# One attention and feed-forward kernel, its commands split finer and their order and engines set anew

## The chip, the cores and the metric

The kernel runs on one core of one Trainium2 chip. The metric is the device time of one execution in microseconds (us), lower is better. A profiled execution gives a span, from the first to the last instruction, and a trace of every instruction and DMA packet.

The engines have queues of their own and each works in order: TensorE (PE, with weight loads listed apart as PEld), VectorE (DVE), ScalarE (ACT), GpSimd (POOL) and SyncE (SP), which only issues DMAs. POOL issues DMAs too: those that convert float32 to float16 on the way.

## The reference, cut to what matters

```python
# q, k, v: (4 batches, 8 heads, 768 tokens, 64) float32; is_retrieval = [1,0,1,0,0,0,1,0]
scores = q @ k.T / 8                       # per batch and head
mask = causal                              # retrieval heads
mask = causal & (first 4 keys | last 64 keys)   # the other heads
a = softmax(where(mask, scores, -1e9))
x = (a @ v), heads side by side            # (3072 tokens, 512)
h = max(x @ w1, x @ w2, x @ w3)            # 512 -> 768
out = h @ w_out                            # 768 -> 512, float32
```

## The kernel before

The work is cut by batch `b` (4) and half of the tokens (2 halves of 384): eight chunks. A chunk has two attention groups `t` of four heads (`t = 4b + 2*half + qd`), each of two pairs `i` of heads. After both groups of a chunk its feed-forward part (FFN) may run: 18 products (three weights, six column blocks, four matmuls each) and 3 output groups.

The order is written out by hand. `PROGRAM` is a list of short commands, which a loop at the end of the kernel runs through; each puts its instructions on the queues of its engines, and nothing reorders them afterwards. Data dependences become semaphore waits. So a command's place sets its place in each queue that it touches, and a letter in it chooses the engine: `d` DVE, `a` ACT, `p` POOL. The commands:

- `hl half hp n ss`: loads K and Q of `n` head pairs of batch 0 as float32 (line 187, two heads each DMA), on SP. `load_v b half` loads V in three DMAs on SP (287). `load b qd` loads K and Q of four heads of a later batch on POOL, to float16 (251). `w i` loads a weight (403, 410) on POOL; w0 comes in two halves.
- `cast half hp` turns batch 0's K and Q of a pair to float16 (212); `turnp` transposes them on PE (231) and copies them out of PSUM (239). For later batches `turn b qd i part` transposes K (`i` = 0) or Q (1) on DVE (267), four commands for each four heads.
- `v t i`: casts V of a pair to `va` (504) and writes `vf`, V times the retrieval flag of its head (506). For far key blocks the product takes `vf`, which is zero for a head that doesn't see them.
- `s t u`: scores of a unit `u` (553; two units in a first half, four in a second; for batch 0 often one pair at a time) and the exponential on ACT (564), which writes `pt`. The scores' PSUM has two buffers `sps`. In `t` 0 and 1 masks are added by matmuls with the identity (537).
- `k t i u`: multiplies the diagonal blocks of `pt` by a mask table (586). `em` and `m` write these tables (389), `flags`, `read` and `far` the flags of the heads.
- `av t i`: A times V (602), then reciprocal (610) and scaling (612) on DVE. With `D` the result is transposed by a DMA on SP (621); otherwise `x t i` does it on PE and copies it (638). The `x` of a chunk's last pair also puts its FFN in the queue.
- `f n`: the next step of the FFN at the head of the queue: one product (438) with its eviction (copy 455 on the engine named if it is the first weight's, else a maximum on DVE, 458), or one output group (474), copied on the engine named (480) and stored (481). Behind each output group the generator yields twice, so the second `f` there does nothing.
- `idle n`: matmuls on zeros at the start; `gate`: SP waits for a piece of `pt`.

All PSUM tiles but the scores' share four buffers ("bank") in turn: a product's fifth successor there waits until its own eviction is done.

Batch 0's order, in words: loads, casts and transposes of pairs as they come; `t` 0 and 1; then the FFN of its first half from 23.6 us, mixed with `t` 2 and 3; then `s 4 0`, the first scores of batch 1.

Of the kernel before, what the change touches and what calls it, by code (L numbers as in the profile page):

```python
# [10 lines left out]
FP16 = mybir.dt.float16  # L11
# [32 lines left out]
FIRST = "hl 0 0 1, ir"  # L44

PROGRAM = (
    "idle 2, idle 8, cast 0 0 aa, hl 0 1 1 ss, hl 0 2 2 ss, read, hl 1 0 2 ss, cast 0 1 pp",
    "flags, cast 0 2 ap, em 1, turnp 0 1 a, far, em 0, turnp 0 0 aa, cast 0 3 da, em 2, em 3",
    "load_v 0 0 4 4, s 0 0 1, s 0 0 0, v 1 1 pp, cast 1 1 pa, turnp 0 3 dd, turnp 0 2 da",
    "w 0 2 0, load_v 0 0 0 4, v 0 0 dp, s 1 0 0, w 0 2 1, s 0 1 0 b, hl 1 2 2 ss, s 1 0 1",  # L50
    "cast 1 2 dp, v 1 0 dd, s 0 1 1, s 1 1 0 b, av 0 0, v 0 1 pp, turnp 1 1 a, s 1 1 1",
    "turnp 1 2 aa, x 0 0 a, s 2 0 1, cast 1 0 dp, load_v 0 1, cast 1 3 ad, av 1 1, s 2 1 1",
    "av 1 0, x 1 1 d, av 0 1, turnp 1 0 ad, s 2 2 1, x 1 0 d, s 3 0 0, m 0, w 1, x 0 1 d",
    "s 2 0 0, m 3, m 1, f 1 d, f 1 d, s 2 1 0, s 2 2 0, m 2, f 1 a, f 1 d, k 2 1 2 p, k 2 0 1 d",
    "w 2, f 1 d, s 2 3 1, load 1 0, w 3, k 3 0 0 d, s 3 1 0, f 1 a, s 2 3 0, load 1 1",
    "k 2 0 3 p, k 2 0 2 p, turnp 1 3 dd, k 3 0 1 p, k 2 1 1 d, k 2 1 3 d, f 1 d, f 1 d",
    "v 2 0 ad, f 1 a, f 1 a, v 3 1 pp, f 1 d, s 3 0 1, v 2 1 dp, s 3 1 1, f 1 a, v 3 0 ap",
    "av 2 0 D, f 1 d, f 1 d, s 3 2 0, turn 1 0 0 0, turn 1 0 0 1, f 1 a, turn 1 0 1 0, s 3 2 1",
    "s 3 3 0, k 3 0 2 p, k 3 1 2 p, turn 1 0 1 1, f 1 a, av 2 1 D, s 3 3 1, k 3 1 1 d",
    "k 3 0 3 p, k 3 1 3 p, f 1 a, k 3 1 0 d, load_v 1 0, gate, f 1 a, s 4 0, k 4 1 0 p",  # L60
    "v 4 0 pp, av 3 0, av 3 1, f 1 a, f 1 a, x 3 0 d, s 4 1, turn 1 1 0 1, x 3 1 a, f 1 d",
    "v 5 1 pp, turn 1 1 1 0, turn 1 1 1 1, turn 1 1 0 0, k 4 0 1 d, k 4 0 0 d, k 4 1 1 p, f 1 a",
    "f 1 a, f 1 d, load_v 1 1, f 1 a, f 1 a, f 1 a, v 4 1 pd, f 1 a, f 1 d, s 5 0, f 1 a, f 1 d",
    "av 4 0 D, k 5 0 0 d, f 1 d, s 5 1, k 5 0 1 p, load_v 2 0, f 1 a, f 1 a, load 2 0, f 1 a",
    "s 6 0, f 1 d, av 4 1 D, f 1 a, v 5 0 ap, f 1 a, s 6 1, f 1 a, av 5 0 D, f 1 d, f 1 d",
    "k 5 1 1 p, k 5 1 0 p, v 7 0 dp, s 6 2, k 6 1 2 p, f 1 a, av 5 1 D, turn 2 0 1 0, f 1 a",
    "v 6 0 ad, s 6 3, turn 2 0 0 1, x 5 1 d, f 1 a, turn 2 0 1 1, load 2 1, load 3 1",
    "load_v 2 1, v 6 1 ap, f 1 d, f 1 d, k 6 0 2 p, v 9 0 ap, k 6 1 3 p, f 1 a, f 1 a",
    "turn 2 0 0 0, s 7 0, f 1 a, f 1 d, f 1 d, turn 2 1 0 0, k 6 0 1 d, f 1 a, s 7 1, f 1 d",
    "f 1 a, f 1 a, k 6 1 1 p, k 7 1 1 d, f 1 d, s 7 2, f 1 a, f 1 a, k 6 0 3 p, k 7 1 2 d",  # L70
    "turn 2 1 1 0, load 3 0, av 6 0 D, s 7 3, f 1 d, v 7 1 pp, av 6 1 D, k 7 1 3 p, f 1 d",
    "turn 3 1 1 0, k 7 0 3 p, turn 2 1 0 1, s 8 0, k 7 0 1 p, turn 2 1 1 1, k 7 0 2 p, f 1 a",
    "f 1 d, load_v 3 0, k 8 0 0 p, av 7 1 D, s 8 1, f 1 a, f 1 a, s 9 0, v 8 0 ap, k 8 0 1 d",
    "f 1 a, f 1 d, av 7 0 D, v 13 1 pp, s 9 1, f 1 a, av 8 0 D, f 1 d, s 10 0, f 1 a, x 7 1 d",
    "f 1 a, v 10 0 dd, f 1 d, s 10 1, f 1 a, f 1 d, v 9 1 ad, f 1 a, f 1 d, f 1 a, s 10 2",
    "f 1 d, f 1 d, f 1 d, k 8 1 0 p, f 1 d, k 9 0 0 p, k 9 1 1 d, f 1 d, f 1 d, v 11 0 ad",
    "f 1 d, k 9 1 0 p, v 12 0 ad, k 9 0 1 p, k 8 1 1 d, av 9 0 D, v 8 1 ap, s 10 3, f 1 d",
    "f 1 a, av 8 1 D, turn 3 0 1 0, s 11 0, k 10 1 1 p, f 1 d, f 1 d, k 10 0 3 p, f 1 a",
    "av 9 1 D, v 13 0 ap, f 1 a, k 10 1 3 d, turn 3 0 1 1, x 9 1 a, k 10 0 1 p, s 11 1, f 1 a",
# [30 lines left out]
def kernel(  # L110
# [68 lines left out]
    def load_pairs(half, hp, n, engines):  # L179
        for nm, src, eng in zip(("ks", "qs"), (k, q), engines):  # L180
            st = (
                pairs2.tile([P, 4, HB, D], FP32, tag=nm, name=nm) if n == 2
                else once.tile([P, 2 * n, HB, D], FP32, name=f"{nm}{hp}")
            )
            m = 2 * n if eng is nc.gpsimd else 2
            for h in range(0, 2 * n, m):
                eng.dma_start(  # L187
                    out=st[:, h : h + m],
                    in_=src[
                        0, 2 * hp + h : 2 * hp + h + m, half * HALF : (half + 1) * HALF  # L190
                    ].rearrange("h (p j) d -> p h j d", p=P),
                )
            for i in range(n):
                staged.setdefault((half, hp + i), []).append(st[:, 2 * i : 2 * i + 2])

    def load_cast(half, hp, n):
        for nm, src in (("kc", k), ("qc", q)):
            st = half16.tile([P, 4, HB, D], FP16, tag=nm, name=nm)
            nc.gpsimd.dma_start(
                out=st[:, 0 : 2 * n],  # L200
                in_=src[
                    0, 2 * hp : 2 * hp + 2 * n, half * HALF : (half + 1) * HALF
                ].rearrange("h (p j) d -> p h j d", p=P),
            )
            for i in range(n):
                cast.setdefault((half, hp + i), []).append(st[:, 2 * i : 2 * i + 2])

    def cast_pair(half, hp, engines):
        cast[half, hp] = []
        for nm, src, op in zip(("kn", "qn"), staged.pop((half, hp)), engines):  # L210
            x = half16.tile([P, HB, 2, D], FP16, tag=nm, name=nm)
            op(out=x, in_=src.rearrange("p h j d -> p j h d"))
            cast[half, hp].append(x)
# [6 lines left out]
    def turn_pair(half, hp, *engines):  # L220
        if (0, hp // 2) not in KQs:
            KQs[0, hp // 2] = qkt.tile([P, 2, S, 2], FP16, tag="KQ", name="KQ")
        xs = cast.pop((half, hp))
        n = 2 // len(engines)
        for part, op in enumerate(engines):
            tr = bank([P, 1024], FP16, "tr")
            for i in range(n):
                for j in range(HB):
                    c, x = i * HALF + j * P, xs[part + i]
                    if x.shape[1] == HB:  # L230
                        nc.tensor.transpose(
                            tr[:, c : c + P], x[:, j].rearrange("p h d -> p (h d)"), ident
                        )
                        continue
                    for h in range(2):
                        nc.tensor.transpose(
                            tr[D * h : D * h + D, c : c + P], x[:, h, j], ident
                        )
# [60 lines left out]
    def load_first(half, hp, n, e="sc"):  # L299
        by = {"s": nc.sync, "c": nc.scalar}  # L300
        load_pairs(half, hp, n, [by[x] for x in e])
# [414 lines left out]
```

## Time and profile before

| | |
|---|---|
| three runs | 200.95 us median (199.65, 200.95, 203.45) |
| the profiled execution | span 199.9 us; its last store is under way from 197.2 |
| PE, DVE, ACT, POOL busy | 190.0, 148.3, 115.9, 90.5 us |
| masks (line 586) | POOL 54, 57.3 us; DVE 32, mean 522 ns (512 elements) and 281 ns (256) |
| exponentials (line 564) | 98, 83.3 us on ACT |
| batch 0's first exponential | 9.85 us |
| first FFN product | 23.64 us |
| `s 4 0` on PE | 43.32 us |
| DMA engines busy, 5 to 45 us | all 16, nearly throughout |

The span is what the sum below is made against. Busy times are of single engines and overlap; an engine off the chain that ends last may stand idle at no cost. In the slices of the span each digit is a fortieth, 5 us, in tenths of busy time. Matmuls are pipelined: one of 384 columns is listed with 327 ns, but four in a row take 650 ns.

### The profile page before, as it was taken

The numbers are of one execution on the slowest core, as the hardware profiler recorded it, in microseconds if no ns is written. First come the engines' busy times: TensorE is split into PE (matmuls) and PEld (weight loads), VectorE is DVE, ScalarE is ACT, GpSimd is POOL, SyncE is SP. The second block draws the span as 40 slices with busy tenths as digits, with TensorE's granted clock in tenths as the row PEclk, the third lists the DMA queues.
The fourth block names the chain that finished last, engine by engine and source line by source line (L and its number), as shares of the span: only waits on it lengthen the run. The fifth ranks groups of instructions, "written<-read, shape, count | busy, mean of one in ns | idle before, by whom it ended". The sixth has DMA issues, their size and how long they took to land.

```text
span 199.9 us, 5135 instructions
## 1 busy us (share of the span) xinstructions
PE 190.0 (95%) x2059; PEld 109.3 (55%) x2059; DVE 148.3 (74%) x311; ACT 115.9 (58%) x171; POOL 90.5 (45%) x118
## 2 busy tenths in 40 slices
PE   7688898999999999999999999999999999999993
PEld 2345444565556455666456645574656455765552
DVE  3638965998976789896469998996978288767750
ACT  4489983765658798687776756634366565100011
POOL 3429187583276598490697245652010197000000
PEclk9889999999999999999999999999999999999999
DMA  5999999995979989988521232703500120124004
GB/s 143 312 245 230 196 195 212 208 169 76 283 173 211 162 169 208 218 218 176 147 76 23 43 124 74 159 20 73 167 5 20 53 108 0 23 59 157 3 0 157
DMA packets 48429, 26.48 MB, mean 132 GB/s; under 512 B 36758, under 2 KB 43926, under 8 KB 48406
## 3 DMA queue, kind: packets, MB, share of 16 engines
q1 hardware_dynamic: 43366, 17.96, 37.9%
q0 software_dynamic: 4624, 7.87, 21.9%
q8 instruction: 16, 0.26, 0.6%
q10 hardware_dynamic: 416, 0.33, 0.5%
q14 instruction: 7, 0.06, 0.1%
HBM read 25.17 MB, written 6.29 MB: 157 GB/s over the span
## 4 chain that ended last, share of the span: by engine, by line
PE 75%; DMA 11%; DVE 4%; SPq 3%; issue 2%; ACT 2%; POOL 0%; DVEq 0%
PE yy L438 39%; PE yy L474 14%; PE st L553 9%; PE oacc L602 9%; DMA vs<-in_v_dram 7%; PE yst L438 3%; DMA qs<-in_q_dram 2%; DVE KQ L267 2%; SPq L187 2%; ACT pt L564 1%; DMA xT<-x 1%; PE yst L474 1%; DVE acc L458 1%; DVE hT L458 1%; SPq L621 1%
## 5 line engine op out<-in xcount | busy, mean ns | idle before, releaser
L564 ACT ACTIVATE pt<-st 128x1024 f16<-128x1024 f32 (+3 forms) x98 | 83.3, 905 | 33.0 <-PE st L553 31.0
L586 POOL TENSOR_TENSOR pt<-pt,mk 128x512 f16<-128x512 f16 (+1 forms) x54 | 57.3, 1088 | 38.4 <-ACT pt L564 20.1
L438 PE MATMUL yy<-xT,w1t 128*128 128x384 f16 x180 | 35.8, 327 | 1.2 <-DVE pt L586 1.2
L438 PE MATMUL yy<-xT,w2t 128*128 128x384 f16 x180 | 36.1, 326 | 0.0
L438 PE MATMUL yy<-xT,w0t 128*128 128x384 f16 x180 | 35.8, 327 | 0.3
L458 DVE TENSOR_TENSOR acc<-yy,acc 128x384 f16<-128x384 f32 x45 | 24.8, 557 | 10.7 <-PE yy L438 8.6
L474 PE MATMUL yy<-woutt,hT 128*128 128x512 f16 (+1 forms) x138 | 31.6, 375 | 0.0
L553 PE MATMUL st<-KQ 32*128 32x384 f16 (+5 forms) x560 | 29.4, 281 | 1.4 <-ACT pt L564 0.8
L458 DVE TENSOR_TENSOR hT<-yy,acc 128x384 f16<-128x384 f32 x45 | 24.8, 556 | 4.5 <-PE yy L438 2.3
L602 PEld LDWEIGHTS <-pt 128*128 128x128 f16 x672 | 24.4, 97 | 4.8 <-DVE va L504 0.7
L267 DVE STREAM_TRANSPOSE KQ<-kq 128x384 f32<-128x384 f32 x24 | 25.5, 1132 | 0.6 <-DMA kq<-in_q_dram 0.6
L602 PE MATMUL oacc<-va,pt 128*128 128x65 f16 x352 | 24.9, 193 | 0.5 <-DVE va L504 0.5
L438 PEld LDWEIGHTS <-w1t 128*128 128x128 f16 x192 | 17.5, 98 | 14.1 <-issue 1.6
L438 PEld LDWEIGHTS <-w0t 128*128 128x128 f16 x192 | 17.8, 98 | 13.4 <-issue 0.8
L438 PEld LDWEIGHTS <-w2t 128*128 128x128 f16 x192 | 17.3, 98 | 11.9 <-issue 1.4
L553 PEld LDWEIGHTS <-KQ 32*128 32x128 f16 (+1 forms) x560 | 12.2, 93 | 18.8 <-issue 11.8
L474 PEld LDWEIGHTS <-hT 128*128 128x128 f16 x150 | 13.8, 98 | 14.7 <-issue 0.8
L602 PE MATMUL oacc<-vf,pt 128*128 128x65 f16 x320 | 21.1, 193 | 0.0
L455 ACT CAST acc<-yy 128x384 f16<-128x384 f32 x25 | 12.0, 481 | 13.9 <-PE yy L438 13.5
L612 DVE TENSOR_TENSOR x<-oacc,rc 128x384 f16<-128x384 f32 x32 | 17.8, 557 | 1.1
L480 DVE COPY ot<-yy 128x512 f32<-128x512 f32 (+1 forms) x15 | 10.1, 675 | 9.2 <-PE yy L474 9.2
L506 POOL TENSOR_TENSOR vf<-va,far 128x384 f16<-128x384 f16 x10 | 8.6, 867 | 17.3 <-ACT va L504 12.9
(72 smaller groups left out, 143.4 us busy)
## 6 DMA issues: line engine op xcount, KB each, us to landing
out_dram<-ot SPq DMA_DIRECT2D x23, 256.0 KB, 2.1
vs<-in_v_dram SPq DMA_DIRECT2D x21, 256.0 KB, 5.6
kq<-in_k_dram POOLq DMA_DIRECT2D x6, 384.0 KB, 7.9
kq<-in_q_dram POOLq DMA_DIRECT2D x6, 384.0 KB, 10.0
ks<-in_k_dram SPq DMA_DIRECT2D x8, 192.0 KB, 3.6
qs<-in_q_dram SPq DMA_DIRECT2D x7, 192.0 KB, 4.8
vs<-in_v_dram SPq DMA_DIRECT2D x6, 128.0 KB, 4.8
w0t<-in_moe_w_dram POOLq DMA_DIRECT2D x2, 384.0 KB, 9.4
```

Source lines behind the costliest of these rows:

```text
L267: nc.vector.transpose(out=dst.rearrange("c (p j) -> c j p", j=n)[:, j0:j1], in_=src.rearrange("c (j i) -> c j i", i=R),)
L438: nc.tensor.matmul(yy[:, 0:HALF], w_t[wi][:, ks, ni * P : (ni + 1) * P], xT[b, half][ks].rearrange("p a t -> p (a t)"), start=(ks == 0), s ...
L455: copy_out[0](out=acc[ni], in_=yy[:, 0:HALF])
L458: nc.vector.tensor_tensor(out=dst, in0=yy[:, 0:HALF], in1=acc[ni], op=ALU.max)
L474: nc.tensor.matmul(yo[:, 0:n], hT[ns][:, tb * P : (tb + 1) * P], woutt[:, ns, c : c + n], start=(ns == 0), stop=(ns == NNB - 1),)
L480: op(out=ot[:, c : c + n], in_=yo[:, 0:n])
L506: vf_engine.tensor_tensor(out=vf[j][:, hs, k0:k1, 0:D], in0=vs[:, hs, 0:1] if half == 0 else va[j][:, hs, k0:k1, 0:D], in1=far[:, hs, k0:k ...
L553: nc.tensor.matmul(sts[g // m][:, g % m, c0 : c0 + n * P], KQ[rows, 0, ki * P : (ki + 1) * P], KQ[rows, 1, t0 : t0 + n * P], start=(c0 == ...
L564: nc.scalar.activation(out=pts[t, i][:, u, h0 : h0 + m, 0:w], in_=st[:, :, 0:w], func=AF.Exp, scale=sc,)
L586: engine.tensor_tensor(out=x, in0=x, in1=m, op=ALU.mult)
L602: nc.tensor.matmul(o[:, qi, hl, 0 : D + 1], pt[:, u, hl, c : c + P], vv[:, 2 * hp + hl, ki, 0 : D + 1], start=(idx == 0), stop=(idx == len ...
L612: nc.vector.tensor_tensor(out=x, in0=o[:, :, :, 0:D], in1=rc.unsqueeze(3).to_broadcast([P, HB, 2, D]), op=ALU.mult,)
```

## The change

Loads and casts of batch 0 are now one command for K (0) or Q (1): `hl half hp n i s`, `cast half hp i engine`. `v` only casts V; the new `vf t i engine` writes the scaled copy. `k t i n` handles one entry `n` of the list of masks, where `u` named the unit after which one or two of them became due. The second yield behind an output group is gone, and with it 24 `f` commands. The first loads stand outside the list, unchanged (K of pair 0 on SP, Q on ACT's queue, then the flags). All commands are in a new order, and many have another engine. Options that the list did not use are removed.

The old list up to `s 5 0`, then the new one up to there, and the functions that differ:

```diff
...
-FIRST = "hl 0 0 1, ir"
 PROGRAM = (
-    "idle 2, idle 8, cast 0 0 aa, hl 0 1 1 ss, hl 0 2 2 ss, read, hl 1 0 2 ss, cast 0 1 pp",
-    "flags, cast 0 2 ap, em 1, turnp 0 1 a, far, em 0, turnp 0 0 aa, cast 0 3 da, em 2, em 3",
-    "load_v 0 0 4 4, s 0 0 1, s 0 0 0, v 1 1 pp, cast 1 1 pa, turnp 0 3 dd, turnp 0 2 da",
-    "w 0 2 0, load_v 0 0 0 4, v 0 0 dp, s 1 0 0, w 0 2 1, s 0 1 0 b, hl 1 2 2 ss, s 1 0 1",
-    "cast 1 2 dp, v 1 0 dd, s 0 1 1, s 1 1 0 b, av 0 0, v 0 1 pp, turnp 1 1 a, s 1 1 1",
-    "turnp 1 2 aa, x 0 0 a, s 2 0 1, cast 1 0 dp, load_v 0 1, cast 1 3 ad, av 1 1, s 2 1 1",
-    "av 1 0, x 1 1 d, av 0 1, turnp 1 0 ad, s 2 2 1, x 1 0 d, s 3 0 0, m 0, w 1, x 0 1 d",
-    "s 2 0 0, m 3, m 1, f 1 d, f 1 d, s 2 1 0, s 2 2 0, m 2, f 1 a, f 1 d, k 2 1 2 p, k 2 0 1 d",
-    "w 2, f 1 d, s 2 3 1, load 1 0, w 3, k 3 0 0 d, s 3 1 0, f 1 a, s 2 3 0, load 1 1",
-    "k 2 0 3 p, k 2 0 2 p, turnp 1 3 dd, k 3 0 1 p, k 2 1 1 d, k 2 1 3 d, f 1 d, f 1 d",
-    "v 2 0 ad, f 1 a, f 1 a, v 3 1 pp, f 1 d, s 3 0 1, v 2 1 dp, s 3 1 1, f 1 a, v 3 0 ap",
-    "av 2 0 D, f 1 d, f 1 d, s 3 2 0, turn 1 0 0 0, turn 1 0 0 1, f 1 a, turn 1 0 1 0, s 3 2 1",
-    "s 3 3 0, k 3 0 2 p, k 3 1 2 p, turn 1 0 1 1, f 1 a, av 2 1 D, s 3 3 1, k 3 1 1 d",
-    "k 3 0 3 p, k 3 1 3 p, f 1 a, k 3 1 0 d, load_v 1 0, gate, f 1 a, s 4 0, k 4 1 0 p",
-    "v 4 0 pp, av 3 0, av 3 1, f 1 a, f 1 a, x 3 0 d, s 4 1, turn 1 1 0 1, x 3 1 a, f 1 d",
-    "v 5 1 pp, turn 1 1 1 0, turn 1 1 1 1, turn 1 1 0 0, k 4 0 1 d, k 4 0 0 d, k 4 1 1 p, f 1 a",
-    "f 1 a, f 1 d, load_v 1 1, f 1 a, f 1 a, f 1 a, v 4 1 pd, f 1 a, f 1 d, s 5 0, f 1 a, f 1 d",
...
+    "hl 0 2 2 0 s, cast 0 0 1 p, idle 8, read, flags, cast 0 0 0 a, hl 0 2 2 1 s, turnp 0 0 da",
+    "em 0, hl 0 1 1 1 s, hl 1 2 2 0 s, em 3, cast 0 2 0 d, cast 0 3 1 d, cast 0 3 0 p",
+    "cast 0 2 1 p, idle 2, em 1, s 0 0 0, turnp 0 3 ad, turnp 0 2 aa, em 2, hl 1 2 2 1 s, s 1 0 1",
+    "cast 0 1 1 p, cast 1 2 0 d, s 1 0 0, cast 1 3 1 p, s 0 1 0 b, cast 1 3 0 d, load_v 0 0 0 4",
+    "hl 0 1 1 0 s, cast 1 2 1 d, hl 1 0 2 0 s, load_v 0 0 4 4, v 0 1 p, hl 1 0 2 1 s, s 1 1 1",
+    "turnp 1 2 ad, m 3, far, cast 0 1 0 p, load_v 0 1, turnp 1 3 ad, cast 1 1 0 d, v 0 0 d",
+    "s 3 0 0, vf 0 0 d, cast 1 0 1 p, s 3 2 0, cast 1 1 1 p, m 0, cast 1 0 0 d, s 3 1 0, s 3 3 0",
+    "w 0 2 0, v 1 0 a, turnp 0 1 d, v 1 1 p, s 1 1 0 b, vf 0 1 d, m 2, turnp 1 0 aa, s 0 0 1",
+    "turnp 1 1 d, s 0 1 1, vf 1 0 p, av 0 0, load 1 0, s 2 0 0, av 0 1, s 3 0 1, vf 1 1 p",
+    "k 3 0 0 p, av 1 0, k 3 0 2 p, v 2 0 p, w 0 2 1, av 1 1, s 2 3 0, s 2 2 0, x 1 0 d, s 3 2 1",
+    "x 0 0 d, x 0 1 d, v 3 0 d, x 1 1 d, w 1, s 2 1 0, s 3 1 1, k 2 0 2 d, f 1 a, k 2 0 1 d",
+    "k 3 0 3 d, turn 1 0 0 1, k 3 1 0 d, k 2 0 0 d, v 3 1 p, vf 2 0 p, m 1, k 3 0 1 d, vf 3 0 p",
+    "vf 3 1 p, s 3 3 1, v 2 1 a, turn 1 0 1 0, f 1 a, turn 1 0 1 1, f 1 a, k 3 1 2 p, s 2 0 1",
+    "k 3 1 3 d, w 2, s 2 1 1, k 3 1 1 d, av 2 0 D, av 3 0, w 3, f 1 a, s 2 3 1, s 2 2 1, gate",
+    "turn 1 0 0 0, f 1 d, vf 2 1 d, f 1 a, av 3 1, x 3 0 a, s 4 0, k 2 1 0 p, f 1 d, k 2 1 1 d",
+    "f 1 d, k 2 1 2 p, f 1 a, f 1 a, s 4 1, f 1 d, f 1 a, k 4 1 2 p, x 3 1 d, f 1 d, k 4 1 1 p",
+    "f 1 d, f 1 a, f 1 a, f 1 a, av 2 1 D, f 1 a, f 1 a, load_v 1 0, f 1 a, f 1 a, load 1 1",
+    "turn 1 1 0 0, f 1 a, turn 1 1 0 1, k 4 0 0 d, turn 1 1 1 1, k 4 0 1 d, f 1 a, f 1 d",
+    "turn 1 1 1 0, k 4 1 0 d, v 5 0 p, f 1 d, f 1 a, f 1 a, s 5 0, f 1 d, f 1 d, load_v 1 1",
...
-    def cast_pair(half, hp, engines):
-        cast[half, hp] = []
-        for nm, src, op in zip(("kn", "qn"), staged.pop((half, hp)), engines):
-            x = half16.tile([P, HB, 2, D], FP16, tag=nm, name=nm)
-            op(out=x, in_=src.rearrange("p h j d -> p j h d"))
-            cast[half, hp].append(x)
+    def cast_pair(half, hp, i, op):
+        nm = ("kn", "qn")[i]
+        x = half16.tile([P, HB, 2, D], FP16, tag=nm, name=nm)
+        op(out=x, in_=staged.pop((half, hp, i)).rearrange("p h j d -> p j h d"))
+        cast[half, hp, i] = x
...
                 eng.dma_start(out=out[r0 : r0 + P, c : c + n], in_=ot[:, c : c + n])
             yield
-            yield
...
-    def prep_v(t, i, op, vf_engine):
+    def cast_v(t, i, op):
+        b, half, qd = where(t)
+        k0 = half * HB
+        hs = slice(4 * qd + 2 * i, 4 * qd + 2 * i + 2)
+        op(out=va[b % 2][:, hs, k0 : k0 + HB, 0:D], in_=staged_v[b, half][:, hs])
+
+    def scale_v(t, i, vf_engine):
         b, half, qd = where(t)
         vs = staged_v[b, half]
-        j, k0 = b % 2, half * HB
+        j = b % 2
         hs = slice(4 * qd + 2 * i, 4 * qd + 2 * i + 2)
-        vdst = va[j][:, hs, k0 : k0 + HB, 0:D]
-        op(out=vdst, in_=vs[:, hs])
         k0, k1 = ((0, 1), (1, 4))[half]
         vf_engine.tensor_tensor(
...
-        for at, u0, nu, cols, n, m0 in APART if t in (3,) else MASKED[half]:
-            if at != u:
-                continue
-            m = mk[:, h0 : h0 + 2, m0 : m0 + n]
+        _, u0, nu, cols, n, m0 = (APART if t in (3,) else MASKED[half])[u]
+        m = mk[:, h0 : h0 + 2, m0 : m0 + n]
...
```

## The prediction

> **What bounds the kernel now.** I read the page's busy rows and slices first, to see which engine is full and where it is not.
>
> ```profile
> span 199.9 us, 5135 instructions
> PE 190.0 (95%) x2059; PEld 109.3 (55%) x2059; DVE 148.3 (74%) x311; ACT 115.9 (58%) x171; POOL 90.5 (45%) x118
> PE   7688898999999999999999999999999999999993
> DMA  5999999995979989988521232703500120124004
> ```
>
> PE is full from the tenth slice (45 us) to the last. Only the first nine have holes, and there the DMA engines are full. Then the chain that ended last, for the points where this turns:
>
> ```profile
> 3.70 4.98 DMA qs<-in_q_dram
> ...
> 15.53 14.68 DMA vs<-in_v_dram
> ...
> 43.32 0.63 PE st L553 x16
> 43.95 1.98 PE oacc L602 x60
> 45.94 1.29 PE yy L474 x6
> ...
> 196.73 0.42 DVE ot L480
> ```
>
> Up to 43 us it runs over loads (V's second half is 14.7 us under way) and evictions; from 43.32, the start of `s 4 0` (first scores of batch 1), nearly all of it is PE. So time = arrival at `s 4 0` + PE's queue behind it + 3.2 of last copy and store. PE's queue, priced from the chain's pieces (product of four matmuls 0.65, output group 1.29, scores of a unit 0.57, 0.45 or 0.34, A times V 0.37 or 0.94, turn of x 0.25), is 149.4; the trace took 196.7 - 43.3 = 153.4. I use 1.0255 for the ratio: a product that follows scores costs 0.11 more (0.76 against 0.65).
>
> Third, stretches and single instructions for the prices:
>
> ```profile
> 5.00:8.40 3.40, 1.52 (x17) 0.98 (x16) 1.81 (x9) 0.85 (x2) 0.93 (x2) 0.96 1.01 303
> 8.40:11.80 3.40, 3.40 (x29) 2.01 (x28) 2.37 (x7) 3.40 (x6) 1.34 (x3) 0.53 1.18 289
> 28.80:32.30 3.50, 2.28 (x19) 1.25 (x18) 2.16 (x5) 2.12 (x4) 1.64 (x3) 1.00 1.16 209
> ```
>
> ```profile
> 73.51 3.38 POOL L586 TENSOR_TENSOR pt<-pt,mk 128x512 f16<-128x512 f16 x3
> 76.41 0.76 DVE L586 TENSOR_TENSOR pt<-pt,mk 128x512 f16<-128x512 f16 x1
> 112.14 0.42 DVE L586 TENSOR_TENSOR pt<-pt,mk 128x512 f16<-128x512 f16 x1
> ```
>
> ```profile
> kq<-in_k_dram POOLq DMA_DIRECT2D x6, 384.0 KB, 7.9
> kq<-in_q_dram POOLq DMA_DIRECT2D x6, 384.0 KB, 10.0
> ```
>
> In the first fence PE's busy time stands behind the length, the clock third from the end: after a stretch with PE 1.52 of 3.40 busy the next runs at 0.53; after 2.28 of 3.50 it does not.
>
> **What the change does, priced.** The 24 empty fills issue nothing: zero. All other work stays and moves. Masks: POOL 54 to 41, DVE 32 to 45. V's casts: ACT 18 to 7, POOL 9 to 15, DVE 5 to 10. Scaled copies: POOL 21 to 17, DVE 11 to 15. K and Q casts: ACT 6 to 1, POOL 6 to 8, DVE 4 to 7. By row means (DVE mask 0.522 or 0.281, cast 0.424 and 0.54, scaled copy 0.35 or 0.737) DVE gains 9.5 us, less four output copies already taken off; ACT loses 7.5, POOL 11.0. DVE would stand near 157 of 200: no bound over the whole, so places decide.
>
> *Arrival at `s 4 0`.* K of pair 0 is cast on ACT at 3.99 as now, Q on POOL (landed by 4.41) to 5.0; six transposes to 5.4, DVE's copy 0.55, two mask tables 0.61, then mask and score matmuls 0.50 + 0.39: first exponential at 7.5, now 9.85. From there to the exponential of `s 2 2 1`, which frees the PSUM that `s 4 0` needs, ACT holds 16 x 1.028 + 4 x 0.811 + 2 x 0.597 + 4 x 0.409 + 7 copies x 0.497 + 2 V casts x 0.516 + 4 evictions x 0.481 = 29.0, less 39 x 0.055 because back-to-back instructions overlap (three in 2.94): 26.8. ACT without a wait: 34.3. DVE is later: the four evictions of `av 0 0` to `av 1 1` follow the exponential of `s 0 1 1` (22.3) and end near 25.2; then 4 copies x 0.35, a cast 0.42, masks 4 x 0.522 + 3 x 0.281, tables 0.77, four `turn` x 1.132, two evictions x 0.745 = 11.5, less overlap 1.2: 35.5, and about 1.5 of waits (an exponential, K and Q of batch 1). I take **37.0**, 6.3 earlier than 43.32. Bounds: 34.3 (ACT alone) and 39.0 (0.1 to 0.2 for each of some ten hand-overs between engines that I left out).
>
> The loads allow this. SP's queue issues the same loads at the same 0.4 to 0.75 each, K and Q one by one, and V's second half last, near 14.5 to 17.3. The weights (0.81 to 0.93 of POOL per issue, as now) sit behind `cast 1 1 1 p`, which waits for the last Q (landing 17.7 by SP's pace): `w 0 2 0` at 18.3 instead of 14.93, its first use 28 instead of 23.6; landing takes 8.7 to 10.0. `w 0 2 1` and `w 1` (25) stand behind `load 1 0` and `v 2 0 p`, and are used at 33.5 and 37; w1's 12.2 us is just enough. `w 2` and `w 3` (31) are used at 42 and 47. No wait is charged; the rival below prices it.
>
> *PE's queue behind `s 4 0`.* 138 products are left instead of 126, one A times V fewer (0.94) and one turn of x fewer (0.25): 156.0 against 149.4, with the ratio **+6.8**. This takes back the whole earlier arrival.
>
> *`load 1 1`.* Now at 28.0, long ahead; in the new order it sits on POOL behind `k 4 1 2 p` and `k 4 1 1 p`, which wait for the exponential of `s 4 1` (ends 41.8): issued 43.6 and 44.2. `turn 1 1 0 0` on DVE waits for K; behind it on DVE stand the other turns and two evictions of the second FFN's products, and behind the fourth turn `s 5 0` on PE, due at 55.05. DVE needs 5.6 from K's landing to the fourth turn. Landed after 5.3 (shortest) the loss is 0.35, after 7.9 (median) 2.0. Only w3 is ahead in POOL's queue and SP holds no load then, so I take 6.6: **+0.8**.
>
> *DVE's heavier stretches.* Four PSUM banks let DVE fall 2 to 2.6 us behind. Adding up its work between two evictions against PE's in the same part of the order, the old order never exceeds this; the new one does where PE has 54 to 56 us of its priced queue behind it (by up to 0.4) and again at 115 to 119 (up to 0.5): **+0.9**, bounds 0 and 2.0.
>
> Here a rule of the Trainium skill speaks against the change. A DVE mask took 0.42 with POOL idle and 0.76 while POOL ran masks. SBUF — State Buffer, "Who interferes with whom", says that a DVE instruction with two SBUF inputs and a GpSimd one that reads SBUF exclude each other, the later one waiting until the first ends. By it, as an estimate, 45 masks with POOL busy 40% of the time and half of 1.15 to wait lose 10 us of DVE time, before 8 (32 masks, 45%): 2 us more on DVE, most of it off PE's path. The rows agree in direction; the row mean of 0.522 already holds part.
>
> **Sum.** 199.9 - 6.3 + 6.8 + 0.8 + 0.9 = 202.1. The runs' median, 200.95, is 1.05 above this execution, the lowest 0.25 below; I add 0.4: **202.5**. Two per cent (196.9 to 205.0) is about what a measurement of this kernel tells from no change: my forecast is inside.
>
> **Rivals.**
> 1. *Slower: `load 1 1` is late.* Place and queue as above. Each us beyond 7.9 costs a us; it decides from a landing of about 9: at 10.0, Q's median, the loss is 4.2, so 205.9. For: medians of 7.9 and 10.0, one took 20.6, and turns, evictions and scores all stand behind one wait. Against: 5.3 was reached. Chance 0.18.
> 2. *Slower: V's second half is late again.* It took 14.7; then `v 2 0 p` holds POOL until 32, `w 0 2 1` is issued at 32.5 and lands at 41, 7 after its use at 34: 209. For: that row. Against: then weights were in flight beside it, in the new order only `w 0 2 0`. Chance 0.13.
> 3. *PE falls to the half clock in the front.* Between 12 and 22 us PE mostly waits for exponentials. A stretch with 1.52 of 3.40 was followed by 0.53, one with 2.28 was not; I count about 2.0. Each stretch of 3.4 at half speed costs up to 1.7 where PE is full: 202.5 + 1.7 = 204.2, two of them 205.9. Chance 0.08, most of it slower. The Trainium skill, TensorE: Matmul & The Clock Gate, Part 1, gives a free-running window of 3413 ns after which an idle array drops to half; the row agrees in length. By it the `idle 2` that now falls into 5.0 to 8.4 would keep the next window at full clock.
> 4. *Faster: nothing waits.* Arrival 34.3, no loss at `load 1 1` or on DVE: 34.3 + 160.0 + 3.2 = 197.5; with the ratio 1.02, 196.6. For: earlier start, even ACT load. Against: it needs ACT without a gap for 27 us. Chance 0.12.
> That the order does not do what it says is no rival: every command is counted.
>
> **Numbers.** Forecast 0.49, rivals 0.18, 0.13, 0.08, 0.12. Faster by over 2%: two thirds of rival 4, 0.08. Slower: rivals 1, 2 and 0.05 of 3, 0.36. Within: 0.49 + 0.03 + 0.04 = 0.56. Range: low 197.5 (rival 4), high 208.0 (rival 1 with 12 us; most of rival 2 is left out); the forecast's own is 199.5 to 205.0.
>
> **What would show it.** First exponential near 7.5; `s 4 0` between 35 and 39; K of batch 1's second half landing near 50, a DVE wait on it of 1 to 3 us and PE's next scores about 1 late; PE full from 38 to the end but for two short holes; 3.2 at the end. Wrong if `s 4 0` comes after 40, if PE waits for w0 or w1, if the clock falls below 1 after 12 us, or if DVE's masks average over 0.6.

## The result, and the profile after

| | median of its runs, us | range of the runs |
|---|---|---|
| before | 200.5 | 199.65 to 203.45 (4) |
| after | 207.45 | 206.91 to 208.01 (4) |

The ratio is 1.033, with an interval of 1.027 to 1.039: the change makes the kernel slower, by more than 2%. I had put 202.5 and "within 2%". The time lies in the range that I gave, in its upper tenth, but not for the reason that set the upper end: that was `load 1 1` landing late, which did not come. The profiled execution has a span of 206.3 where I had summed 202.1. The page of the kernel after, its busy rows and three of its slice rows:

```profile
span 206.3 us, 5132 instructions
...
PE 192.6 (93%) x2059; PEld 110.5 (54%) x2059; DVE 160.1 (78%) x334; ACT 109.9 (53%) x157; POOL 80.9 (39%) x109
...
PE   7779878999999999989799999899999999999993
...
PEclk9996996999999999999999999999999999999999
DMA  5999999919999989999780240013502130114004
```

PE's row now has 8s and a 7 behind the tenth slice; before, it had none. So the first thing to read is what PE waits for there. PE's waits from 40 us on, kernel after (us in total, times, longest):

```profile
PE yy L411 <- DMA xT<-x: 1.3, 2, 1.2
PE yy L411 <- DVE acc L428: 0.9, 1, 0.9
PE yy L411 <- DVE acc L431: 0.3, 1, 0.3
PE yy L411 <- DVE hT L431: 0.3, 1, 0.3
PE oacc L576 <- DVE pt L560: 0.3, 1, 0.3
PE st L529 <- DVE KQ L249: 0.2, 1, 0.2
PE oacc L576 <- DVE x L586: 0.2, 1, 0.2
```

The same view of the kernel before, from 44 us on, is empty. Six of the seven rows name DVE as the late one, by way of an eviction, a mask, a transposition or the scaling of `x`; the first names the DMA transpose of `x`, which nothing in my sum had priced. The timeline of PE shows where they lie (start, length, operation, and in brackets the idle time ahead of it and what ended it), with the start of `s 4 0` as the second row:

```profile
31.63 0.20 PE L576 MATMUL oacc<-va,pt 128*128 128x65 f16 x1 [1.33 <-DVE pt L560]
...
38.42 0.63 PE L529 MATMUL st<-KQ 32*128 32x384 f16 x16
...
73.48 0.65 PE L411 MATMUL yy<-xT,w0t 128*128 128x384 f16 x3 [0.18 <-DMA xT<-x]
...
85.49 0.81 PE L411 MATMUL yy<-xT,w2t 128*128 128x384 f16 x4 [0.34 <-DVE acc L431]
...
94.36 0.63 PE L529 MATMUL st<-KQ 32*128 32x384 f16 x16 [0.25 <-DVE KQ L249]
...
101.13 0.65 PE L411 MATMUL yy<-xT,w0t 128*128 128x384 f16 x3 [1.17 <-DMA xT<-x]
...
133.20 0.81 PE L411 MATMUL yy<-xT,w0t 128*128 128x384 f16 x4 [0.94 <-DVE acc L428]
```

Three places, then: 1.4 us by which `s 4 0` is later than forecast; holes of 1.24 between 85 and 95 with 1.17 for x at 101; holes of 0.94 and 0.23 at 133 and 136. With 0.18 at 73 the holes are 3.76.

Behind the first and the third place stands the same picture on DVE. Its timeline, with POOL's row at the same time below it:

```profile
25.96 4.13 DVE L560 TENSOR_TENSOR pt<-pt,mk 128x512 f16<-128x512 f16 x3
...
127.00 0.41 DVE L560 TENSOR_TENSOR pt<-pt,mk 128x512 f16<-128x512 f16 x1
127.33 1.12 DVE L249 STREAM_TRANSPOSE KQ<-kq 128x384 f32<-128x384 f32 x1
...
129.88 1.38 DVE L560 TENSOR_TENSOR pt<-pt,mk 128x512 f16<-128x512 f16 x1
131.18 1.50 DVE L482 TENSOR_TENSOR vf<-va,far 128x384 f16<-128x384 f16 x1
```

```profile
25.49 2.53 POOL L482 TENSOR_TENSOR vf<-va,far 128x384 f16<-128x384 f16 x3
...
127.01 6.68 POOL L560 TENSOR_TENSOR pt<-pt,mk 128x512 f16<-128x512 f16 x5 [8.67 <-issue]
```

A mask of the same size on DVE takes 0.41 as POOL's burst begins and 1.38 in the middle of it; a scaled copy, 0.53 at 78.1 with POOL idle, takes 1.50. POOL's own masks pay too: 1.34 each in the burst, 1.15 alone. DVE's transposition, which has one input, keeps its 1.12. At the second place DVE and POOL also run side by side from 85 to 95, and there another thing stands ahead of it, V of batch 2:

```profile
84.04 0.94 DVE L474 CAST va<-vs 128x384 f16<-128x384 f32 x2 [1.44 <-DMA vs<-in_v_dram]
...
84.06 0.69 POOL L474 CAST va<-vs 128x384 f16<-128x384 f32 x1 [8.45 <-DMA vs<-in_v_dram]
...
85.62 4.72 POOL L560 TENSOR_TENSOR pt<-pt,mk 128x512 f16<-128x512 f16 x4
```

POOL stands 8.45 us for V (`v 8 1 p`) and then does four masks in a row.

### The profile page after: what moved, and what is told of

It reads as the page before. It is cut to its first block, busy times and chain, and to the rows that moved or that the text cites. A ratio compares the mean times of both kernels' runs of the same rounds, so it can differ in the third digit from the quotient of the medians.

```text
span 206.3 us, 5132 instructions
## 1 busy us (share of the span) xinstructions
PE 192.6 (93%) x2059; PEld 110.5 (54%) x2059; DVE 160.1 (78%) x334; ACT 109.9 (53%) x157; POOL 80.9 (39%) x109
## 4 chain that ended last, share of the span: by engine, by line
PE 58%; DVE 15%; DMA 14%; ACT 4%; issue 4%; SPq 2%; POOL 1%; DVEq 0%; ACTq 0%
PE yy L411 28%; PE yy L447 9%; DMA vs<-in_v_dram 8%; PE oacc L576 7%; PE st L529 6%; DMA kq<-in_k_dram 4%; DVE pt L560 4%; ACT pt L540 4%; PE yst L411 3%; DMA xT<-x 2%; DVE KQ L249 2%; PE st L295 2%; DVE vf L482 2%; DVE acc L431 2%; PE tr L218 1%
## 5 line engine op out<-in xcount | busy, mean ns | idle before, releaser
L560 POOL TENSOR_TENSOR pt<-pt,mk 128x512 f16<-128x512 f16 (+1 forms) x41 | 45.4, 1123 | 63.7 <-ACT pt L540 53.3
L411 PE MATMUL yy<-xT,w0t 128*128 128x384 f16 x180 | 36.7, 331 | 2.3 <-DMA xT<-x 1.3
L411 PE MATMUL yy<-xT,w2t 128*128 128x384 f16 x180 | 35.6, 327 | 0.3 <-DVE acc L431 0.3
L249 DVE STREAM_TRANSPOSE KQ<-kq 128x384 f32<-128x384 f32 x24 | 26.2, 1126 | 1.2 <-DMA kq<-in_k_dram 0.6
L560 DVE TENSOR_TENSOR pt<-pt,mk 128x512 f16<-128x512 f16 (+1 forms) x45 | 22.3, 509 | 1.1 <-ACT pt L540 1.1
L428 ACT CAST acc<-yy 128x384 f16<-128x384 f32 x24 | 11.5, 488 | 19.8 <-PE yy L411 19.5
L576 PE MATMUL oacc<-vf,pt 128*128 128x65 f16 x320 | 21.6, 195 | 0.2 <-DVE x L586 0.2
L453 ACT COPY ot<-yy 128x512 f32<-128x512 f32 x12 | 7.1, 588 | 19.3 <-PE yy L447 18.5
```

The source lines that it names most:

```text
L249: nc.vector.transpose(out=dst.rearrange("c (p j) -> c j p", j=n)[:, j0:j1], in_=src.rearrange("c (j i) -> c j i", i=R),)
L411: nc.tensor.matmul(yy[:, 0:HALF], w_t[wi][:, ks, ni * P : (ni + 1) * P], xT[b, half][ks].rearrange("p a t -> p (a t)"), start=(ks == 0), s ...
L428: copy_out[0](out=acc[ni], in_=yy[:, 0:HALF])
L453: op(out=ot[:, c : c + n], in_=yo[:, 0:n])
L560: engine.tensor_tensor(out=x, in0=x, in1=m, op=ALU.mult)
L576: nc.tensor.matmul(o[:, qi, hl, 0 : D + 1], pt[:, u, hl, c : c + P], vv[:, 2 * hp + hl, ki, 0 : D + 1], start=(idx == 0), stop=(idx == len ...
```

## The experiments

Each is an edit of the command list of the kernel named; its ratio is to the kernel before, run beside it. The last two columns are of one profiled execution each. The expectations call an attention group `t` a tile.

| kernel | ratio | interval | `s 4 0` in its profile | wait for x near 73 |
|---|---|---|---|---|
| after | 1.033 | 1.027 to 1.039 | 38.42 | 0.18 |
| `load_v 2 0` one step up | 1.029 | 1.024 to 1.034 | 38.39 | 0 |
| front copies on DVE | 1.031 | 1.025 to 1.036 | 36.53 | 2.60 |
| mid copies on POOL | 1.028 | 1.023 to 1.033 | 37.45 | 0 |
| these three edits | 1.021 | 1.015 to 1.026 | 36.20 | 2.38 |
| three edits, `av 4 1` earlier | 1.017 | 1.013 to 1.021 | 36.97 | 0.77 |
| three edits, V ahead of x | 1.060 | 1.055 to 1.064 | 36.66 | 7.02 |
| both | 1.059 | 1.054 to 1.064 | 36.39 | 6.47 |
| before, three x in a row | 1.045 | 1.040 to 1.049 | 41.31 | 7.09 |
| after, V's casts later | 1.033 | 1.027 to 1.038 | 37.63 | 2.33 |
| three edits, x by PE | 1.011 | 1.008 to 1.014 | 36.96 | 0 |
| that, and tiles 6, 7 | 1.011 | 1.009 to 1.013 | 36.89 | 0 |

**1. Is it V?** `e1`, on the kernel after:

```diff
-av 5 1 D, f 1 a, av 5 0 D, av 4 1 D, x 5 1 d, s 6 2, turn 2 1 0 1, f 1 d, load_v 2 0
+av 5 1 D, f 1 a, av 5 0 D, av 4 1 D, load_v 2 0, x 5 1 d, s 6 2, turn 2 1 0 1, f 1 d
```

> The changed kernel with one edit: the load of V of batch 2 (first half) is put on SP's queue ahead of the four DMA transposes of x behind A times V of tiles 4 and 5, so it is issued near 59 instead of 72.7 to 79.2. Theory Q (V arrives late at 83.9, DVE waits 1.4 for it, POOL 8.5, then both catch up and PE runs dry five times from 85 to 95 and once for xT at 101, 2.4 us in all): V lands before 75, the POOL wait is gone, PE's holes from 85 to 102 shrink from 2.4 to under 0.8, time falls by 1.5 to 2.5 us, to about 205.4. Rival, theory L (DVE is simply overfull between 84 and 97, whatever V does): the holes stay, time within 0.5 us of the changed kernel's. A third way: V in flight beside K and Q of batch 2 delays their turns at 69.6, and PE waits there: 1 to 4 us slower.

The edit did less than I wrote: the transposes of x are issued by the `av ... D` commands, not by `x 5 1 d`, so V passed one output store only and was issued at 71.97 instead of 72.75. DVE's wait for V fell from 1.44 to 0.3, POOL's from 8.45 to 7.0, PE's holes from 85 to 90 were gone, those at 90 to 93 stayed (0.46). The gain, 0.4 points of the ratio, is inside the intervals. In its profiled execution x came 3.09 late at 102, which the kernel after doesn't show, so its span (210.0) doesn't tell what the edit is worth.

**2. The front: contention, or DVE's amount of work?** `e2`, on the kernel after, gives DVE three instructions more:

```diff
-v 3 1 p, vf 2 0 p, m 1, k 3 0 1 d, vf 3 0 p, vf 3 1 p
+v 3 1 p, vf 2 0 d, m 1, k 3 0 1 d, vf 3 0 d, vf 3 1 d
```

> The changed kernel with the scaled copies of V for tiles 2 (pair 0) and 3 (both pairs) on DVE instead of POOL: DVE has three instructions more in the front, about 1.6 us at the 0.53 that one took alone. Theory C (DVE operations with two SBUF inputs and POOL's hold each other up: three DVE masks took 4.13 us beside POOL's three scaled copies and a mask, 0.42 each where POOL is idle): the three masks at 26 us take 1.3 to 2.0, PE's wait of 1.33 before oacc at 31.6 is gone, DVE is through this part 0.5 to 1.5 us earlier in spite of the added work, first scores of batch 1 (s 4 0) near 37.5 instead of 38.4, time 0.5 to 1.5 us lower. Rival, theory L (DVE's amount of work sets it): 1.6 us more on DVE, s 4 0 near 40, time 1 to 1.6 us higher.

DVE and PE in its timeline:

```profile
25.59 2.24 DVE L560 TENSOR_TENSOR pt<-pt,mk 128x512 f16<-128x512 f16 x3
...
30.43 1.01 DVE L482 TENSOR_TENSOR vf<-va,far 128x384 f16<-128x384 f16 x2
```

```profile
36.53 0.63 PE L529 MATMUL st<-KQ 32*128 32x384 f16 x16
...
74.02 1.12 PE L411 MATMUL yy<-xT,w0t 128*128 128x384 f16 x3 [2.60 <-DMA xT<-x]
```

With more to do DVE is done sooner: the three masks take 2.24 instead of 4.13 (one POOL mask still runs beside them), and `s 4 0` starts 1.9 earlier. That is contention, and the theory of DVE's amount falls. Not all of the 1.9 is contention, though: the kernel after ran two stretches of the front at half clock, `e2` none (the clock is taken up below). The ratio moves by 0.2 points only. In the profiled execution the 1.9 us come back as a wait of 2.60 for x at 74. This execution is long for `e2`, with a span of 206.9; four others have 204.1 to 204.9 and one has 207.2. Whether x is as late in the shorter ones isn't known, since they were not profiled.

**3. The holes at 133.** `e3`, on the kernel after:

```diff
-k 10 1 0 p, f 1 d, vf 10 0 p
+k 10 1 0 p, f 1 d, vf 10 0 p, vf 11 1 p, vf 10 1 p
...
-vf 11 1 d, k 11 1 1 d, s 11 3, vf 10 1 d
+k 11 1 1 d, s 11 3
```

> The changed kernel with two scaled copies of V (tiles 10 and 11, pair 1; 0.55 and 1.50 on DVE at 129.4 and 131.2, beside a burst of five POOL masks) put on POOL right behind the scaled copy at 117.4, where POOL is idle for 8.7 us. Theory: DVE is the late one there: PE's two holes at 133 and 135 (0.94 and 0.23) go, and time falls by 1.0 to 1.3 us, to about 206.3. Rival: PE's hole moves on to the next late item behind it (av of tile 10), and time stays within 0.4.

Both holes are gone, and the ratio falls by 0.5 points, about what was forecast, though the intervals overlap. POOL ran the copies at 116.6 to 119.1, where it had stood idle. A DVE mask beside POOL's burst still takes 1.39 (at 126.17); without the two copies DVE can afford it.

**4. The three together.** `e4` is the edits of 1, 2 and 3 in one list.

> The three edits together. If the three places are separate: the sum of the three gains, 3 to 5 us, so 202.5 to 204.5. If one hole just moves into the next late item, less than the largest single gain plus 0.5.

1.021: 2.4 us (1.2 points) below the kernel after, about the sum of the three (1.1). The time, 205.1, is above the 202.5 to 204.5 that I had put, since the single gains were smaller than forecast. It is the only one of the four whose interval lies clear of that of the kernel after. The chain of waits of this kernel names what is left:

```profile
66.70 0.25 DVE x L586
...
68.87 0.02 SPq L595
68.88 0.03 issue
68.91 4.52 DMA xT<-x
73.43 0.04 issue
73.47 0.65 PE yy L411 x3
```

The last of three A times V in a row (`av 5 1 D`, `av 5 0 D`, `av 4 1 D`) has its x at 67.26 (the scaling takes 0.56 in all, of which the chain shows 0.25). SP, which issues one transpose in about 1.2 (the one before this took 2.11), comes to it at 68.9, and it lands 4.52 later. PE has about 5 us of other work between that A times V (to 65.8) and the product that reads it (begun at 70.8).

**5. Bunching, V ahead of x, and the same on the kernel before.** Four kernels: `g1`, `g2` and `g3` on the three edits, `g4` on the kernel before.

`g1`, one of the three A times V earlier:

```diff
-av 4 0 D, f 1 d, s 6 0, f 1 a, k 5 0 1 d
+vf 4 1 d, av 4 0 D, f 1 d, s 6 0, f 1 a, av 4 1 D, k 5 0 1 d
...
-k 5 1 1 d, f 1 a, vf 4 1 d, k 5 0 2 d
+k 5 1 1 d, f 1 a, k 5 0 2 d
...
-av 5 0 D, av 4 1 D, load_v 2 0, x 5 1 d
+av 5 0 D, load_v 2 0, x 5 1 d
```

`g2`, V where the kernel before has it (`g3` has the edits of both):

```diff
-k 5 1 2 d, f 1 a, av 4 0 D
+k 5 1 2 d, f 1 a, load_v 2 0, av 4 0 D
...
-av 4 1 D, load_v 2 0, x 5 1 d
+av 4 1 D, x 5 1 d
```

`g4`, the kernel before with three in a row:

```diff
-s 6 0, f 1 d, av 4 1 D, f 1 a, v 5 0 ap, f 1 a, s 6 1, f 1 a, av 5 0 D, f 1 d, f 1 d
+s 6 0, f 1 d, f 1 a, v 5 0 ap, f 1 a, s 6 1, f 1 a, f 1 d, f 1 d
...
-k 6 1 2 p, f 1 a, av 5 1 D
+k 6 1 2 p, f 1 a, av 4 1 D, av 5 0 D, av 5 1 D
```

> The kernel with the three edits, and in it A times V of tile 4, pair 1 is moved some 6 us of PE work earlier (its scaled copy of V too), so that two instead of three DMA transposes of x are issued in a row ahead of the feed-forward products of batch 1's second half. Theory B (bunching: three transposes in a row take SP 1.2 each and land 6 us after the last A times V, while PE has 4.9 us of other work until the product that needs them): PE's hole of 2.4 near 73.5 shrinks to 0.5 to 1.5, time 1 to 2 us below the three edits alone, ratio to before near 1.013. Rival D (the DMA engines are full there whatever the order, the last transpose lands near 73.4 in any case): the hole stays over 2 us and the time within 0.5.

> The kernel with the three edits, but the load of V of batch 2 (first half) goes where the kernel before had it: right behind the load before it on SP, ahead of all four transposes of x of tiles 4 and 5 (in the earlier edit it only passed one output store). Issued near 57 instead of 70. Theory Q (V too late for DVE and POOL): no wait for V at 82, PE's holes between 90 and 96 (0.55) and its wait for x at 100 (0.9) go, 1 to 1.5 us faster. Rival D (DMA engines full from 50 to 74): V's 768 KB, some 4 us at 200 GB/s, now stands ahead of K, Q and x, the hole at 73.5 grows from 2.4 by 1 to 4 us, and time stays or rises by up to 3 us.

> Both of the last two edits on top of the three (V of batch 2 early, A times V of tile 4, pair 1 early). If B and Q hold: 2 to 3.5 us below the three edits alone, near 1.005 of before. If D holds: no better than the three edits alone.

> The kernel before with one edit the other way: A times V of tile 4 (pair 1) and of tile 5 (pair 0) are moved back to just ahead of that of tile 5 (pair 1), so that three transposes of x stand in a row as in the changed kernel. Theory B: PE, which had no hole there, waits 1.5 to 2.5 us for the last transpose near 73, and the time rises by 1.5 to 2.5 us (ratio 1.008 to 1.012). Rival D: the last transpose lands when it did, PE waits under 0.5, time within 0.5.

`g1` goes the way of bunching, but weakly. The wait shrinks from 2.38 to 0.77, but `s 4 0` is 0.77 later in this profile, which takes about as much off the wait by itself, and the last transpose lands only 0.5 earlier (72.95 for 73.43). So the rival, that it lands near 73.4 in any case, isn't excluded. In time the edit is worth 0.4 points, within the intervals and less than the 1 to 2 us that I had put.

`g2` and `g3` went the rival's way, and further than I put it: with V's load ahead of x the waits near 73 are 7.02 and 6.47 (in `g3` up to 78.6), and both kernels lose some 8 us. In `g2` SP issues V from 57.2, its third piece alone holds SP for 6.99, V lands from 70.07 to 71.93, and the first of the four transposes, issued at 66.35, lands at 73.32. The Trainium skill, DMA: Bandwidth & Descriptors, "Queues, rings and completion order", says that on each DMA engine the descriptors of a queue are consumed in ring order. These landings agree with that. So the late V of the kernel after was the price of an early x, not an oversight.

`g4` shows that three in a row cost time in the kernel before too. That kernel has V ahead of three of its four transposes and no wait; its four A times V stand 3 to 5 us of PE work apart. Put three in a row, and the last transpose lands 10 us after its issue. The chain of `g4`:

```profile
66.00 0.57 DVE x L612
66.57 1.11 SPq L621
...
67.77 10.03 DMA xT<-x
77.79 0.04 issue
77.83 4.32 PE yy L438 x13
```

I had forecast 1.5 to 2.5 us for it; it costs 9: waits of 7.09, and a clock of 0.50 to 0.65 from 72 to 84 behind them. V doesn't set this size. V of batch 2 landed at 67.03, before SP issued this transpose at 67.77. What is under way then are four loads of K and Q that POOL issued from 66.27 to 67.89; the last of them lands at 77.55, the transpose 0.24 later. In the kernel before the last transpose goes out at 67.87, POOL's loads follow from 68.94, and it lands after 2.51.

In eight traces the Q load ahead of the last of these transposes lands at most 1.3 us after its issue, and its time goes with what comes behind it. Where POOL's next load of K is issued 0.8 to 1.1 us behind this transpose (the kernel after, `e1`, `e3`, the kernel before and its second profile), it lands after 2.3 to 2.6, and PE waits 0.18 at most. Where that load comes 0.6 behind (`e2`, `e4`, `h1`), it lands after 4.4 to 4.8, and PE waits 2.3 to 2.6. The kernel after, `e3` and `h1` have the same commands up to there, and waits of 0.18, 0 and 2.33: the order alone doesn't fix this wait. No run moves POOL's load alone, so that it is the cause is read from the traces, not shown.

**6. V's casts later.** `h1`, on the kernel after:

```diff
-vf 7 1 p, f 1 a, v 8 1 p, load_v 2 1, k 7 1 0 d, s 7 3, v 9 1 d, v 8 0 d
+vf 7 1 p, f 1 a, load_v 2 1, k 7 1 0 d, s 7 3
...
-s 8 0, k 7 0 2 d, k 7 0 0 p, vf 9 0 p
+s 8 0, v 8 0 a, v 9 1 a, k 7 0 2 d, k 7 0 0 p, v 8 1 p, vf 9 0 p
```

> The changed kernel with three of the casts of V of batch 2 moved behind the work that does not need V: the one on POOL behind the masks of tiles 6 and 7, the two on DVE behind the scores of tile 8 and onto ACT. Theory Q (the waits of 1.44 on DVE and 8.45 on POOL for this V make the masks come in a burst from 85 to 95, beside DVE's, and PE runs dry for 1.25 there and 1.17 for x at 101): no wait for V there, the holes between 85 and 102 shrink from 2.4 to under 0.8, and the time falls by 1.2 to 2.2 us (ratio to before 1.022 to 1.027 instead of 1.033). Theory L (DVE is overfull there anyway): DVE is relieved by 0.9 of casts alone, time falls by 0.3 to 0.9. If nothing there counts: within 0.3.

Neither engine waits for V any more, and the holes between 85 and 103 shrink from 2.4 to 1.44, of which 0.98 is x again. The ratio is 1.033 as before, so the gain that I had put didn't come. The smaller holes can't be put down to the edit: in its profile x is 2.33 late at 74.8, which gives V time to land, and `e2`, with x 2.60 late and the casts where they were, has only 1.11 there and no wait of DVE for V. Over the traces the holes at 85 and 90 alone go with DVE's wait for V: 0.68 with a wait of 1.44 (the kernel after), 1.07 with 1.83 (`e3`), none with 0.34 (`e1`). Moving the casts alone buys nothing that can be measured.

**7. x by PE.** `h2`, on the three edits, takes three transposes off the DMA queues:

```diff
-av 5 1 D, f 1 a, av 5 0 D, av 4 1 D, load_v 2 0, x 5 1 d, s 6 2, turn 2 1 0 1, f 1 d, f 1 a
+av 5 1, f 1 a, av 5 0, av 4 1, load_v 2 0, x 5 1 a, s 6 2, x 5 0 a, turn 2 1 0 1, f 1 d, x 4 1 a, f 1 a
```

`h3` adds the casts of `h1` and the last two transposes of tiles 6 and 7:

```diff
-s 8 1, av 7 0 D, av 6 1 D
+s 8 1, av 7 0, av 6 1
...
-s 9 0, k 8 1 1 p, f 1 d, f 1 a
+s 9 0, x 7 0 a, k 8 1 1 p, f 1 d, x 6 1 a, f 1 a
```

> The kernel with the three edits, and three of the four transposes of x of tiles 4 and 5 done on PE with ACT's copies (0.25 of PE and 0.48 of ACT each) instead of by DMA. If PE waits at 73.5 because x's transposes stand in full DMA queues: the hole of 2.4 goes, PE pays 0.75, and V of batch 2 is issued some 3 us earlier and lands earlier: 1.5 to 3 us faster than the three edits alone, ratio to before 1.005 to 1.013. If the feed-forward there is paced by something else (DVE, scores): within 0.7 of the three edits alone, or slower by the 0.75.

> As the one before, and also the casts of V of batch 2 moved back, and the last two transposes of x of tiles 6 and 7 on PE. If each hole found so far is taken away by its own edit: PE without a hole from 37 on but for 0.5, PE's queue 161.3 behind s 4 0, so 36.5 + 161.3 + 3.2 = 201 in the profile, ratio to before 1.000 to 1.008. If a hole moves on to the next late item: no faster than the kernel without these last edits.

PE's waits from 40 on in `h2` are two, and neither names x:

```profile
PE oacc L576 <- DVE pt L560: 0.3, 1, 0.3
PE st L529 <- DVE KQ L249: 0.2, 1, 0.2
```

The wait at 73 is gone, and the one at 101 as well, which the edit doesn't touch: V of batch 2 is issued from 62.7 instead of 70.2, and the two V loads behind it are issued by 84.1, 4.7 ahead of the next transposes (86.4 and 3.3 in the three edits). Whether the wait at 101 hangs on that wasn't tested. The ratio is 1.011, just clear of the three edits alone (1.008 to 1.014 against 1.015 to 1.026): of all that was tried, taking x off the DMA queues is the one step beyond the three edits with a gain that can be measured. `h3` adds nothing: it removes waits that were no longer there. It stays above its forecast (1.011 for 1.000 to 1.008): two holes that name DVE, 0.23 and 0.25 near 91, are left and a new wait of 0.44 for x ahead of its turn on PE has come. No version is faster than the kernel before.

**8. The kernel before once more**, for a second profile.

> The kernel before, unchanged, for a second profile. Its first one had the clock at 0.53 in one stretch (8.4 to 11.8) and s 4 0 at 43.3; the version of it with the bunched transposes had no such stretch and s 4 0 at 41.3. If x's transposes pace the kernel near 72: with s 4 0 near 41.3, PE waits about 1 to 2 us for x between 68 and 75 and the span is within 1 us of 199.9. If not: no hole there, and the span is about 2 us shorter, near 198.

It answers nothing on x: in this execution the last load of V's second half, issued at 15.97, landed 24.7 us later (18.5 in the first profile; the 14.68 of the prediction is the piece that the chain shows), the casts of that half came only at 40.8, PE waited 6.05 at 42.4, and the span was 208.6. It does show how much hangs on that one load.

## Why the prediction was wrong, and where it was right

**The front.** The first exponential came at 7.66 (7.5). Arrival at `s 4 0` was 38.42 for 37.0, inside the bounds. Two things make up the 1.4. One is DVE's masks: I took the row mean of 0.522, and three of them took 4.13 beside POOL's copies. At a like clock, with one stretch at half speed each, `s 4 0` is at 37.45 and 37.63 with that contention (`e3`, `h1`) and at 36.89 to 36.97 without (`g1`, `h2`, `h3`), so it is worth 0.5 to 0.7. The other is the clock: the kernel after has a second such stretch. With the front edited the arrival is 36.2 to 37.0 in seven profiles, so the adding-up of ACT and DVE held. The rule of the Trainium skill that I weighed, SBUF — State Buffer, "Who interferes with whom", agrees with the rows (0.41 alone, 1.38 beside POOL); the wrong step is the sentence that most of it lies off PE's path. The row mean is an average over both cases and fits neither, and a burst on POOL falls exactly where DVE is full.

**PE's queue.** Forecast 160.0 from `s 4 0` to the last product (160.2 in the sum, as 153.4 + 6.8); measured 203.2 - 38.4 - 3.8 of holes = 161.0. The gain in the front is spent on 12 more products behind it, as said; the end is 3.1 for 3.2. `h2` shows the frame alone: 36.96 + 160.0 + 0.75 for the turns on PE + 0.5 of waits + 3.1 = 201.3; its span is 202.0.

**`load 1 1`.** Issued at 45.0, K landed 4.6 later, DVE waited 0.5 and PE not at all: 0 for the 0.8 charged. Rival 1 did not come.

**DVE's heavier stretches.** I charged 0.9 with an upper bound of 2.0; the holes that name DVE are 2.4. The first stretch was in the right place (54 to 56 us of queue behind is 94 to 96, holes at 92 and 94), the second was not: nothing at 160, but 1.17 at 133. There the amount of work would have fitted, and the contention made it not fit: mask and two copies took 3.4 instead of 1.5.

**What was missing.** The step that failed outright is "PE full from 38 on but for two short holes". The change puts three transposes of x in a row ahead of one feed-forward part and two ahead of the next, and moves V of batch 2 behind the first three. I followed K, Q, V and the weights through SP's and POOL's queues, and not x's own DMAs, although each goes through SP and is in flight beside POOL's K and Q. PE waits 1.35 us for x in the profile of the kernel after, and 1.1 to 3.5 in those of `e1` to `e4` and `h1`. With three of these transposes off the DMA queues the wait is gone, and the ratio falls from 1.021 to 1.011. That x's way by DMA costs this is shown; how much of it is the three in a row, and how much the loads beside them, stays open.

**The other rivals.** Rival 2 (V's second half late) did not come: `v 2 0 p` ran at 23.0. Rival 3 came, twice, in the profiled execution:

```profile
11.80:15.20 3.40, 2.29 (x26) 1.40 (x25) 2.60 (x9) 3.40 (x8) 1.32 (x4) 1.00 1.22 272
15.20:18.60 3.40, 2.89 (x20) 1.84 (x20) 2.79 (x9) 3.31 (x7) 1.56 (x3) 0.56 1.29 253
...
28.80:32.30 3.50, 1.67 (x41) 1.22 (x38) 3.50 (x10) 2.85 (x5) 1.97 (x4) 1.00 1.16 207
32.30:35.70 3.40, 3.40 (x43) 1.92 (x39) 3.33 (x8) 0.69 (x2) 1.10 (x1) 0.55 1.16 208
```

(PE's busy time stands behind the length, the clock third from the end.) Its price was below the 1.7 that I put on each. `e4` and `g1` have the same commands up to 50 us: without such a stretch `s 4 0` starts at 36.20, with one (0.67 in 15 to 20) at 36.97, so 0.8; over the seven profiles with the front edited it is 36.20 to 36.66 without and 36.89 to 36.97 with one. Runs of the kernel after with a mean clock of 1.00 and of 0.98 differ by 0.7 in span (205.6 and 206.3); it is a part of the arrival, and too small to make the verdict. Rival 4 did not come.

**The sum, again.** 202.1 + 1.4 of arrival + 3.8 of holes + 0.8 of queue - 1.7 that was charged for `load 1 1` and DVE - 0.1 at the end = 206.3. The class follows from these sizes: 2.4 of holes at DVE and 1.35 at x, where I had 0.9 and nothing. One more term was too small: I added 0.4 for the way from the span to the time of the runs, but the runs with a span on record lie 1.6 to 2.1 above it (208.01 and 206.3 in the kernel after), so a span of 202.1 stands for a time near 203.8, still within 2%. That 207.45 lies inside the range is luck. The forecast's own range ended at 205.0; what stretched it to 208.0 was rival 1, which did not come.

## What to carry to other kernels

Follow every DMA that a moved command issues, the small ones on the tile's way from one engine to another above all: a list of gaps between a producer and the first reader of its transfer, with the length of the queue ahead and the loads that other queues have in flight, would have put this place on the list before the run. Price an operation that shares a resource by two durations, alone and beside the other, and ask which of them holds where the engine is full. And when an edit brings the front forward and the time stays, look for the next thing that doesn't move with it.

## What the runs showed of the hardware that I had not expected

- A DVE operation with two inputs in SBUF, three times as long beside POOL: 1.38 for 0.41 (mask), 1.50 for 0.53 (scaled copy). Not each one in a burst pays: a copy at 129.4, in the same burst, took 0.55. Giving DVE three such copies that POOL had done beside it made DVE earlier, not later.
- A DMA transpose of 128 x 384 values landed after 2.3 us at best, and after 9.6 to 10.4 where POOL had issued loads of K and Q ahead of it, on another queue. It then landed just behind the last Q: at 72.32 after 72.10 in the kernel after, 70.06 after 69.70 in `e4`, 71.86 after 71.51 in `g1`, 77.79 after 77.55 in `g4`.
- Half clock comes in stretches of 3.41 us on one grid (at 15.60 and 32.67 in the kernel after, five such steps apart), so PE's busy share ahead has to be read on the grid's borders. On mine 2.29 of 3.40 was followed by 0.56 in the kernel after, and 2.28 of 3.50 by 1.00 in the kernel before. On the grid 1.53 (the kernel before), 1.58 and 1.90 of 3.41 (the kernel after) were followed by half clock, and 2.08 (`h1`) and 2.19 (the kernel before) were not. In between the share doesn't decide: 1.72 was followed by full clock in `g2`, 2.04 by half clock in `e1`.
